# Attention visits merged to one per head pair inside an FFN's matrix products, and the denominators' sums moved to another PSUM bank

## The chip, the cores and the metric

The kernel runs on one core of a Trainium2 chip. Five engines work on it side by side: TensorE (PE in the profile; its weight loads are PEld), VectorE (DVE), ScalarE (ACT), GpSimd (POOL) and SyncE (SP), which issues nearly all the DMA transfers. The metric is the time of one execution on the device in microseconds, the median of several runs.

## The reference

Two stages follow each other. The first is attention with normalized q and k, for 8 batches, 12 heads, 448 rows and 64 columns a head:

```python
def rmsnorm(x, g):
    rms = np.sqrt(np.mean(x * x, axis=-1, keepdims=True) + 1e-06)
    return x / rms * g
q_n, k_n = (rmsnorm(q, g_q), rmsnorm(k, g_k))
scores = scale * np.matmul(q_n, k_n.transpose(0, 1, 3, 2))      # scale = 1 / 8
scores = scores - np.max(scores, axis=-1, keepdims=True)
attn = np.exp(scores)
attn = attn / (np.sum(attn, axis=-1, keepdims=True) + 1e-09)
attn_out = np.matmul(attn, v)
```

Its output is brought to 3584 rows (batch and row) of 768 columns (head and column) and goes through a feed-forward network (FFN) with squared ReLU; `w_in` is 768x2048, `w_out` 2048x768:

```python
h = np.maximum(x @ w_in, 0.0)
out = h * h @ w_out
```

The kernel computes in 32-bit floating point. The FFN's weights come in 64 bits, and the kernel makes 32-bit values of them on the chip.

## The kernel before

**Pairs.** Heads are taken two at a time, which fills 128 partitions with 2 x 64 columns. There are 8 batches of 6 pairs, 48 pairs in all, numbered `i` from 0. A pair's 448 keys are cut into slots `m`: three of 128 keys, and a last half slot of 64, which an even pair shares with the odd pair after it (so an even pair has four slots to score and an odd one three).

**Work of a pair.** Its steps and lines are:

- q and k are squared (`square`, L179 on ScalarE or L181 on GpSimd), added up (`Rows.add`, L192 and L195, VectorE), brought to the power -1/2 (`power`, L202, GpSimd), and q is scaled (`scale`, L217, GpSimd). The factor of k is applied later, as the scale of the exponential.
- q and k are turned, so that the head's columns lie along the partitions. Early pairs do it on TensorE (`turn`, L357 and L360) into a PSUM bank; VectorE takes q out (L365), ScalarE takes k out (L367). Later pairs read 32x32 blocks through DMA, and VectorE turns them in SBUF (`turn_blocks`, L328); ScalarE multiplies q by the gains (L330).
- `weigh`: the scores of a slot for both heads (L387, TensorE, 64 rows by 128 columns of the array for each head; the half slot uses 64 by 64) go to two of the banks 0 to 3, and ScalarE exponentiates them to SBUF (L392). The softmax works without subtracting the maximum when the gains are small enough; that is the branch that runs here (`shift=False`).
- `attend`: weights times v (L458, 128 rows by 64 columns of the array for each head) is summed in the bank of `values_bank`.
- The denominators are sums over keys. In the first phase TensorE forms them (`add_weights`, L471, 128 by 32). Later GpSimd adds the slots up (`add_up`, L411), and TensorE finishes with two products with ones (`denominators`, L488, 128 by 64). They lie in the bank of `sums_bank`.
- VectorE transposes the denominators (`take_sums`, L499), inverts and spreads them (`invert`, L508 to L515) and multiplies the values by them (`finish`, L527), which gives the FFN's input for this pair.

**Stages.** The FFN takes two batches at once in a Strassen scheme of seven products (`first_products` with L646 and L653, `hidden` with L666 to L668, `second_products` with L698, L727 and L768). There are four such FFNs, called units 1 to 4 here; each has four blocks, and a block consists of two times seven products of the first kind (6 matmuls of 448 columns each) and then the second kind (L698 for the rows left over, then 3 times seven products of 4 matmuls of 384 columns each). The FFN uses banks 5, 6 and 7, in turn.

- The *first phase* computes the pairs of batches 0 and 1 without any FFN work, because no input for one is there yet. The weights are converted to 32 bits and to the forms of the Strassen scheme meanwhile (`convert`, L828 to L887, on ScalarE, VectorE and GpSimd).
- *Unit 1* is mixed with the attention of batches 2 and 3, *unit 2* with batches 4 and 5, *unit 3* with 6 and 7. *Unit 4* runs alone.

**What sets the order.** The whole order is written out by hand: the program is emitted with `manual_schedule`, so each engine works in the order of the code. The main loop takes each pair `i` in two *visits* `n` = 0 and 1. In the first phase a visit is `visit_alone`; in the units it is `visit_among`. Between two visits `run` draws steps of the FFN from a generator until a cost is reached (18 for a first product, 10 for a second; a visit comes at every 24th of a unit), and at each step it takes one or two tasks from a queue (`tasks`, `pool_tasks`) of small work of the other engines. What is left of them is emitted at the start of a visit. A visit works on two pairs: it scores slots of pair `i`, and sums values and denominators of pair `i - 1`:

- `visit_alone`, n = 0: scores of slots 0 and 1 of `i`; turn k, then q, of `i + 1` (banks 7 and 6); squares of `i + 2`; three slots of the values of `i - 1`; two slots of its sums (bank 6).
- `visit_alone`, n = 1: the other scores; the last slot of the values; the other two slots of the sums; then `take_sums`, `invert` and `finish`.
- `visit_among`: n = 0 and n = 1 have two slots of values and two slots of scores each, and n = 1 has the denominators (bank 3) ahead of them. From pair 14 on the turn is made by blocks, as two tasks of which one comes ahead of each visit.

A bank with two uses makes a wait: the second writer waits until the first use was read. In the first phase bank 6 serves both the turned q of `i + 1` and the sums of `i - 1`.

Of the kernel before, what the change touches and what calls it, by code (L numbers as in the profile page):

```python
# [21 lines left out]
P = 128  # L22
# [201 lines left out]
def program(ctx, tc, rows, v, g, wide, ones, moe_w_in, moe_w_out, out, shift):  # L224
# [45 lines left out]


    def slots_of(i, n):

        return [m for m in (2 * n, 2 * n + 1) if m < NJ + 1 - i % 2]
# [77 lines left out]
    def turn(i, x):  # L352

        tr = banks[6 + x if i < 2 or alone(i - 2) else 0]
        dst = att.tile([P, S], F32, name="qT" if x == 0 else "kT")
# [22 lines left out]

    def weigh(i, m):

        scs = [banks[m % 2 * 2 + e][:, 0:S] for e in range(2)]
        for p in (i, i + 1) if m == NJ else (i,):
            some = ds(p % 2 * LASTS, LASTS) if m == NJ else ds(0, P)
            keys = ds(m * P, LASTS if m == NJ else P)
            for e, sc in enumerate(scs):
                r = ds(e * D, D)
                nc.tensor.matmul(  # L387
                    sc[some], lhsT=turned[p, 1][r, keys], rhs=turned[p, 0][r, :],
                    start=True, stop=True,
                )  # L390
        for e, sc in enumerate(scs):
            nc.scalar.activation(  # L392
                new_weights((i, m), e), sc, AF.Exp,
                scale=rows.rr[i][:, 1, 2 * m + e : 2 * m + e + 1],
            )
# [46 lines left out]
    def sums_bank(i):  # L442
        return banks[6 if alone(i) else 3][:, 0:S]

# [537 lines left out]
    def weigh_slots(i, n):  # L982
        if not shift:
            for m in slots_of(i, n):
                weigh(i, m)
        elif n:
            weigh_shifted(i)
# [10 lines left out]
    def visit_alone(i, n):  # L998
        step = i * 2 * VISITS + 2 * n
        if n == 0:  # L1000
            load_v(i)
            if i and shift:
                attend_all(i - 1)
            weigh_slots(i, n)
            turn(i + 1, 1)
            turn(i + 1, 0)
            square(i + 2, 0, new_acc())
# [3 lines left out]
            if i and not shift:  # L1011
                attend(i - 1, range(NJ))
                add_weights(i - 1, (0, 1))
                forget(i - 1, (0, 1))
        else:
# [8 lines left out]
            if i and not shift:  # L1024
                attend(i - 1, (NJ,))
                add_weights(i - 1, (2, 3))
                forget(i - 1, (2, 3))
                take_sums(i - 1)
# [14 lines left out]
    def visit_among(i, n):  # L1043
# [15 lines left out]
        if n and i <= last and not shift:  # L1059
            additions(i)  # L1060
        if n == 0 and i + 2 <= last:
            room = io.tile([P, 4 * P], F32, name="squares", tag="squares", bufs=1)
            square(i + 2, 0, room)
            tasks.append(lambda: None)
            tasks.append(lambda: rows.add(i + 2, 0))
            tasks.append(lambda: square(i + 2, 1, room))
            tasks.append(lambda: rows.add(i + 2, 1))
            tasks.append(lambda: pool_tasks.append(lambda: put_in_order(i + 2)))
            if in_blocks(i + 2):
                tasks.append(lambda: load_blocks(i + 2, 1))  # L1070

    with tc.manual_schedule(engines=ENGINES):
# [8 lines left out]
        for i in range(len(pairs) + 1):  # L1081
            for n in range(VISITS):
                at = i * VISITS + n - VISITS - unit
# [4 lines left out]
                if x == 0:  # L1088
                    u, x = u - 1, unit
                run(COST * (2 * x - 1) / (2 * unit))  # L1090
                if i < last:
                    if in_blocks(i + 1):
                        tasks.append(lambda i=i, n=n: turn_blocks(i + 1, 1 - n))
                    else:
                        turn(i + 1, n)
                    if n:
                        tasks.append(lambda i=i: load_qk(i + 4))
# [3 lines left out]
                if x == unit:  # L1101
# [4 lines left out]
                    elif first:  # L1106
                        run(COST_IN + 1)
                visit_among(i, n)
        run(COST)
# [32 lines left out]
```

## Time and profile before

The time before is 1451.85 us, the median of three runs (1451.38 to 1452.49). The profiled execution has a span of 1451.4 us, in which the granted clock of TensorE is 0.999 of full speed.

| stretch, us from the start | what runs | PE busy | DVE busy | ACT busy | POOL busy |
|---|---|---|---|---|---|
| 0 to 140.6 | first phase | 121.7 | 109.4 | 91.3 | 85.2 |
| 140.6 to 503.3 | unit 1, attention of batches 2 and 3 | 359.0 | 245.9 | 194.7 | 217.0 |
| 503.3 to 850.1 | unit 2, attention of batches 4 and 5 | 346.8 | 129.2 | 124.3 | 164.7 |
| 850.1 to 1189.8 | unit 3, attention of batches 6 and 7 | 339.7 | 120.2 | 115.2 | 145.7 |
| 1189.8 to 1446.3 | unit 4 | 255.5 | 69.1 | 59.5 | 31.6 |

A row of a profile's groups has the line of the code, the engine, the operation with what it writes and reads, and how often; in an answer by time the first two numbers are the start and the length in us, and a bracket at the end tells how long the engine had been idle and what released it. Matmuls are pipelined: the recorded length of one contains its run through the array, so a stream of them overlaps, and what one costs is read from the difference between starts. Each matmul instruction of the program stands as two in the trace, so a slot of values for two heads is four rows.

### The profile page before, as it was taken

Reading aid. Unit: us, or ns where it says so; the run is one execution under the profiler, and the core shown is the slowest. Engines: PE = TensorE matmul, PEld = TensorE weight load, DVE = VectorE, ACT = ScalarE, POOL = GpSimd, SP = SyncE. Lnnn points to the kernel's source line nnn. Section 1 sums busy time; section 2 is a strip of 40 time slices with the busy share of each in tenths; the row PEclk is TensorE's granted clock in tenths of the full one; section 3 lists DMA queues with packets and bytes.
Section 4 is the critical chain, followed back from the end, with each engine's and each line's share of the span. In section 5 each row is a group of like instructions: output and inputs, shape, how many; then the busy total and the mean of one; then the engine's idle time right before and its main releaser. Section 6 shows DMA issues by size and latency. Waiting matters only on the chain.

```text
span 1451.4 us, 15319 instructions
## 1 busy us (share of the span) xinstructions
PE 1422.7 (98%) x4932; PEld 680.3 (47%) x4932; DVE 673.8 (46%) x1269; ACT 584.9 (40%) x1102; POOL 644.1 (44%) x568
## 2 busy tenths in 40 slices
PE   7999999999999999999999999999999999999998
PEld 3333444444444445444454444545444455555554
DVE  5898365877768433234352542334234241232313
ACT  5775466647554243432414234352332404222130
POOL 5567654746557545343534645345342422021111
PEclk9999999999999999999999999999999999999999
DMA  5666336665676644525424464343523233223122
GB/s 144 173 190 161 66 96 192 176 193 140 193 202 213 195 127 103 166 74 145 122 64 151 120 189 121 123 100 92 161 66 110 85 120 117 88 76 125 38 87 79
DMA packets 309278, 188.11 MB, mean 130 GB/s; under 512 B 265796, under 2 KB 293316, under 8 KB 300996
## 3 DMA queue, kind: packets, MB, share of 16 engines
q1 hardware_dynamic: 308896, 186.97, 44.2%
q8 instruction: 41, 0.67, 0.2%
q14 instruction: 49, 0.40, 0.1%
q10 hardware_dynamic: 292, 0.07, 0.0%
HBM read 144.57 MB, written 42.40 MB: 129 GB/s over the span
## 4 chain that ended last, share of the span: by engine, by line
PE 93%; DVE 4%; issue 1%; ACT 1%; DMA 1%; POOL 0%; SPq 0%; ACTq 0%; DVEq 0%; POOLq 0%
PE bank L646 35%; PE bank L727 30%; PE bank L387 9%; PE bank L458 9%; PE bank L698 5%; PE bank L488 2%; PE bank L471 1%; DVE few L508 1%; DVE in_sb L865 0%; DVE out_sb L887 0%; DVE inverse L515 0%; DVE in_sb L861 0%; DVE in_sb L841 0%; PE bank L357 0%; DVE qT L365 0%
## 5 line engine op out<-in xcount | busy, mean ns | idle before, releaser
L646 PE MATMUL bank<-xT,in_sb 128*128 128x448 f32 x1344 | 517.5, 542 | 0.0
L646 PEld LDWEIGHTS bank<-xT,in_sb 128*128 128x128 f32 x1344 | 251.7, 190 | 262.4 <-issue 249.4
L768 DVE TENSOR_TENSOR acc<-acc,bank 128x384 f32<-128x384 f32 x324 | 173.7, 549 | 277.0 <-PE bank L727 203.2
L392 ACT ACTIVATE wT<-bank,rr 128x448 f32<-128x448 f32 x288 | 161.5, 633 | 263.9 <-PE bank L387 246.7
L727 PE MATMUL bank<-out_sb,hid 128*128 128x384 f32 x768 | 267.3, 488 | 0.0
L202 POOL TENSOR_TENSOR rr<-ms,minus_half 128x8 f32<-128x8 f32 (+1 forms) x96 | 146.4, 1525 | 249.7 <-DVE ms L195 238.8
L666 DVE TENSOR_TENSOR hid<-bank,part 128x448 f32<-128x448 f32 x128 | 77.0, 622 | 304.1 <-PE bank L646 302.8
L727 PE MATMUL bank<-out_sb,sums 128*128 128x384 f32 x576 | 204.0, 490 | 3.4 <-DVE acc L768 3.3
L727 PEld LDWEIGHTS bank<-out_sb,hid 128*128 128x128 f32 x768 | 144.8, 190 | 106.9 <-issue 6.1
L682 POOL TENSOR_TENSOR sums<-hid 128x384 f32<-128x384 f32 x32 | 32.5, 1016 | 318.2 <-ACT hid L668 318.2
L411 POOL TENSOR_TENSOR sum<-sum,wT 128x448 f32<-128x448 f32 (+1 forms) x144 | 163.6, 1159 | 16.2 <-ACT wT L392 13.8
L387 PE MATMUL bank<-qT,kT 64*128 64x448 f32 (+1 forms) x768 | 163.6, 573 | 1.4 <-DVE qT L365 1.1
L667 ACT ACTIVATE hid<-hid 128x448 f32<-128x448 f32 x128 | 73.4, 574 | 200.4 <-DVE hid L666 200.4
L727 PEld LDWEIGHTS bank<-out_sb,sums 128*128 128x128 f32 x576 | 107.6, 190 | 88.0 <-DVE acc L768 8.4
L653 ACT COPY part<-bank 128x448 f32<-128x448 f32 x128 | 67.9, 530 | 180.0 <-PE bank L646 179.8
L411 POOL TENSOR_TENSOR sum<-wT 128x448 f32<-128x448 f32 x72 | 83.5, 1179 | 71.8 <-PE bank L488 71.8
L458 PE MATMUL bank<-wT,vt 128*64 128x448 f32 x480 | 106.2, 546 | 0.0
L387 PEld LDWEIGHTS bank<-qT,kT 64*128 64x128 f32 (+1 forms) x768 | 55.2, 173 | 106.3 <-issue 86.9
L192 DVE TENSOR_REDUCE ms<-squares 128x8 f32<-128x512 f32 (+1 forms) x68 | 42.0, 617 | 126.3 <-ACT squares L179 126.3
L698 PE MATMUL bank<-out_sb,hid 128*128 128x384 f32 x256 | 86.4, 491 | 0.0
L668 ACT ACTIVATE hid<-hid 128x448 f32<-128x448 f32 x128 | 74.0, 578 | 4.1
L698 PEld LDWEIGHTS bank<-out_sb,hid 128*128 128x128 f32 x256 | 47.6, 190 | 39.3 <-issue 5.7
(83 smaller groups left out, 1135.4 us busy)
## 6 DMA issues: line engine op xcount, KB each, us to landing
out_sb<-out_forms SPq DMA_DIRECT2D x24, 1536.0 KB, 7.6
in_sb<-in_forms SPq DMA_DIRECT2D x24, 1344.0 KB, 5.9
words<-in_moe_w_in_dram SPq DMA_DIRECT2D x32, 384.0 KB, 3.7
words<-in_moe_w_out_dram SPq DMA_DIRECT2D x32, 384.0 KB, 3.6
out_forms<-out_sb SPq DMA_DIRECT2D x8, 1536.0 KB, 6.8
in_forms<-in_sb SPq DMA_DIRECT2D x8, 1344.0 KB, 6.1
qk<-in_q_dram SPq DMA_DIRECT2D x96, 96.0 KB, 3.2
qk<-in_k_dram SPq DMA_DIRECT2D x96, 96.0 KB, 2.7
```

The lines of the kernel that those rows point to most:

```text
L202: self.nc.gpsimd.tensor_tensor(out=self.rr[i][:, x, 0 : self.count(i)], in0=ms, in1=self.minus_half.to_broadcast(list(ms.shape)), op=ALU.pow,)
L387: nc.tensor.matmul(sc[some], lhsT=turned[p, 1][r, keys], rhs=turned[p, 0][r, :], start=True, stop=True,)
L392: nc.scalar.activation(new_weights((i, m), e), sc, AF.Exp, scale=rows.rr[i][:, 1, 2 * m + e : 2 * m + e + 1],)
L411: nc.gpsimd.tensor_tensor(out=sums[i, e][some], in0=left[some], in1=weights[key_of(i, m), e][some], op=ALU.add)
L458: nc.tensor.matmul(values_bank(i)[ds(e * D, D), :], lhsT=lasts[i % 2][mine, e, :] if m == NJ else values[i][:, m, e, :], rhs=weights[key_o ...
L646: nc.tensor.matmul(ps, lhsT=w_sb[:, IN.index(left), c, :], rhs=forms[u, c][right], start=first and c == 0, stop=c == NK - 1, skip_group_ch ...
L666: nc.vector.tensor_tensor(out=dst, in0=left, in1=right, op=op)
L667: nc.scalar.activation(dst, dst, AF.Relu)
L668: nc.scalar.activation(dst, dst, AF.Square)
L698: nc.tensor.matmul(ps, lhsT=flat[a][:, t, ds(NT * P, P)], rhs=w_sb[t][:, 2 * a + half, :], start=(a, t) == parts[0], stop=(a, t) == parts[-1],
L727: nc.tensor.matmul(ps, lhsT=lefts[left][:, t, ts(tt, P)], rhs=w_sb[t][:, OUT.index(right), :], start=first and t == 0, stop=t == 1, skip_g ...
L768: nc.vector.tensor_tensor(out=acc, in0=acc, in1=ps, op=ALU.add)
```

## The change

Four things are changed.

- *From pair 25 on one visit a pair* (`whole`, `visit_whole`), which is from the start of unit 2. The scores of slots 0 and 1 come first, then all values of pair `i - 1`, with the exponentials between them in the order of ScalarE, then the denominators, then the scores of the other slots. The scores lie in banks 0 to 3 in another order (`banks_of`), and the denominators in bank 0. Scoring on TensorE and exponentials are split into `score` and `weigh`. The purpose is that the array's form changes less often.
- *Preparation* (squares, sums of squares, powers, stores of q, loads of blocks) becomes a function, `prepare`, and for the whole visits it is done for pair `i + 3` in place of `i + 2`. The two tasks of the turn come together, half a period ahead of a visit.
- *In the first phase* the sums of a pair lie in the bank of the other parity's values (4 or 5) and no longer in bank 6. TensorE adds them in one group a pair, in the second visit.
- *The order of turning* in the first phase is q and then k, and their banks are 7 and 6.

The diff, cut to its core:

```diff
@@ -269,6 +269,11 @@
+    def whole(i):
+        return i > 2 * 2 * NPAIR
     def slots_of(i, n):
         return [m for m in (2 * n, 2 * n + 1) if m < NJ + 1 - i % 2]
@@ -351,7 +356,7 @@
     def turn(i, x):
-        tr = banks[6 + x if i < 2 or alone(i - 2) else 0]
+        tr = banks[7 - x if i < 2 or alone(i - 2) else 0]
         dst = att.tile([P, S], F32, name="qT" if x == 0 else "kT")
         for j in range(NJ):
             nc.tensor.transpose(
@@ -376,9 +381,14 @@
             weights[n, e] = att.tile([P, S], F32, name="wT", tag="wT", bufs=8)
         return weights[n, e]
-    def weigh(i, m):
-        scs = [banks[m % 2 * 2 + e][:, 0:S] for e in range(2)]
+    def banks_of(i, m):
+        first = 2 * m - 3 if whole(i) and m > 1 else m % 2 * 2
+        return [banks[(first + e) % 4][:, 0:S] for e in range(2)]
+    def score(i, m):
+        scs = banks_of(i, m)
         for p in (i, i + 1) if m == NJ else (i,):
             some = ds(p % 2 * LASTS, LASTS) if m == NJ else ds(0, P)
             keys = ds(m * P, LASTS if m == NJ else P)
@@ -388,7 +398,10 @@
                     sc[some], lhsT=turned[p, 1][r, keys], rhs=turned[p, 0][r, :],
                     start=True, stop=True,
                 )
-        for e, sc in enumerate(scs):
+    def weigh(i, m):
+        for e, sc in enumerate(banks_of(i, m)):
             nc.scalar.activation(
                 new_weights((i, m), e), sc, AF.Exp,
                 scale=rows.rr[i][:, 1, 2 * m + e : 2 * m + e + 1],
@@ -440,7 +453,7 @@
                 nc.vector.tensor_copy(out=tiles[NJ][e][mine, part], in_=tr[mine, NJ, :size])
     def sums_bank(i):
-        return banks[6 if alone(i) else 3][:, 0:S]
+        return banks[4 + (i + 1) % 2 if alone(i) else 0 if whole(i + 1) else 3][:, 0:S]
     def values_bank(i):
         return banks[4 + i % 2 if alone(i) else 4][:, 0:S]
@@ -982,6 +995,7 @@
     def weigh_slots(i, n):
         if not shift:
             for m in slots_of(i, n):
+                score(i, m)
                 weigh(i, m)
         elif n:
             weigh_shifted(i)
@@ -1002,16 +1016,14 @@
             if i and shift:
                 attend_all(i - 1)
             weigh_slots(i, n)
+            turn(i + 1, 0)
             turn(i + 1, 1)
-            turn(i + 1, 0)
             square(i + 2, 0, new_acc())
             square(i + 2, 1, new_acc(), nc.gpsimd)
             begin(step)
             normalize(i + 2, 0)
             if i and not shift:
                 attend(i - 1, range(NJ))
-                add_weights(i - 1, (0, 1))
-                forget(i - 1, (0, 1))
         else:
             weigh_slots(i, n)
             normalize(i + 2, 1)
@@ -1023,8 +1035,8 @@
             load_qk(i + 4)
             if i and not shift:
                 attend(i - 1, (NJ,))
-                add_weights(i - 1, (2, 3))
-                forget(i - 1, (2, 3))
+                add_weights(i - 1, range(NJ + 1))
+                forget(i - 1, range(NJ + 1))
                 take_sums(i - 1)
                 invert(i - 1)
                 finish(i - 1)
@@ -1058,16 +1070,57 @@
             tasks.append(lambda: finish(i - 1))
         if n and i <= last and not shift:
             additions(i)
-        if n == 0 and i + 2 <= last:
-            room = io.tile([P, 4 * P], F32, name="squares", tag="squares", bufs=1)
-            square(i + 2, 0, room)
-            tasks.append(lambda: None)
-            tasks.append(lambda: rows.add(i + 2, 0))
-            tasks.append(lambda: square(i + 2, 1, room))
-            tasks.append(lambda: rows.add(i + 2, 1))
-            tasks.append(lambda: pool_tasks.append(lambda: put_in_order(i + 2)))
-            if in_blocks(i + 2):
-                tasks.append(lambda: load_blocks(i + 2, 1))
+        if n == 0:
+            prepare(i + 2)
+            run_tasks(2)
+            tasks.appendleft(lambda: None)
+        elif whole(i + 1):
+            prepare(i + 3)
+    def prepare(i):
+        if i > last:
+            return
+        room = []
+        tasks.append(
+            lambda: room.append(io.tile([P, 4 * P], F32, name="squares", tag="squares", bufs=1))
+        )
+        for x in range(2):
+            tasks.append(lambda x=x: square(i, x, room[0]))
+            tasks.append(lambda x=x: rows.add(i, x))
+        tasks.append(lambda: pool_tasks.append(lambda: put_in_order(i)))
+        if in_blocks(i):
+            tasks.append(lambda: load_blocks(i, 1))
+    def visit_whole(i):
+        run_tasks(len(tasks) + len(pool_tasks))
+        if i <= last and not shift:
+            for m in slots_of(i, 0):
+                score(i, m)
+        if shift:
+            attend_all(i - 1)
+        else:
+            for n in range(NJ + 1):
+                attend(i - 1, (n,))
+                forget(i - 1, (n,))
+                if i <= last and n < 2:
+                    weigh(i, n)
+            denominators(i - 1)
+        if i <= last:
+            weigh_slots(i, 1)
+            load_v(i)
+        if not shift:
+            tasks.append(lambda: invert(i - 1))
+            tasks.append(lambda: finish(i - 1))
+            if i <= last:
+                additions(i)
+        prepare(i + 3)
+    def turn_among(i, x):
+        if in_blocks(i):
+            tasks.append(lambda: turn_blocks(i, x))
+        else:
+            turn(i, x)
     with tc.manual_schedule(engines=ENGINES):
         if shift:
@@ -1079,7 +1132,7 @@
         if shift:
             rows.scale(1, 1, nc.gpsimd)
         for i in range(len(pairs) + 1):
-            for n in range(VISITS):
+            for n in range(1 if whole(i) else VISITS):
                 at = i * VISITS + n - VISITS - unit
                 if at < 0:
                     visit_alone(i, n)
@@ -1087,13 +1140,11 @@
                 u, x = divmod(at, unit)
                 if x == 0:
                     u, x = u - 1, unit
-                run(COST * (2 * x - 1) / (2 * unit))
+                run(COST * (2 * x - (2 if whole(i - 1) else 1)) / (2 * unit))
                 if i < last:
-                    if in_blocks(i + 1):
-                        tasks.append(lambda i=i, n=n: turn_blocks(i + 1, 1 - n))
-                    else:
-                        turn(i + 1, n)
-                    if n:
+                    for some in (1, 0) if whole(i) else (1 - n,):
+                        turn_among(i + 1, some)
+                    if n or whole(i):
                         tasks.append(lambda i=i: load_qk(i + 4))
                     if n and first and x > 1 and not shift:
                         denominators(i - 1)
@@ -1105,7 +1156,10 @@
                         run(COST)
                     elif first:
                         run(COST_IN + 1)
-                visit_among(i, n)
+                if whole(i):
+                    visit_whole(i)
+                else:
+                    visit_among(i, n)
         run(COST)
         drain()
         for _ in ffn(B // 2 - 1):
```

## Prediction

> **What bounds the kernel now.** I read the busy shares first, then TensorE's waits, then the order of time around the visits that the change touches.
>
> ```profile
> PE 1422.7 (98%) x4932; PEld 680.3 (47%) x4932; DVE 673.8 (46%) x1269; ACT 584.9 (40%) x1102; POOL 644.1 (44%) x568
> ```
>
> TensorE is busy 98% of the span, so only two things can shorten the kernel: the few waits of TensorE, and time that counts as busy but is not needed. TensorE's own list of waits shows the first:
>
> ```profile
> PE bank L471 <- DVE qT L365: 7.5, 5, 1.8
> PE bank L357 <- ACT g L100: 3.5, 1, 3.5
> PE bank L727 <- DVE acc L768: 3.3, 4, 1.3
> ```
>
> The largest item, 7.5 us in 5 waits, is in the first phase (12 pairs, no FFN yet; the first FFN matmul starts at 140.8 us). The sums of a pair (L471) share bank 6 with the turned q of the pair after the next (L357, evacuated by VectorE at L365), and so wait for VectorE. One of the five, and what VectorE does then:
>
> ```profile
> 52.50 0.92 PE L458 MATMUL bank<-acc,vt 128*64 128x448 f32 x4
> 55.17 0.57 PE L471 MATMUL bank<-wT,ones_of 128*32 128x448 f32 x2 [1.75 <-DVE qT L365]
> ```
>
> ```profile
> 54.44 0.67 DVE L365 TENSOR_SCALAR qT<-bank,g 128x448 f32<-128x448 f32 x1
> ...
> 59.88 0.65 DVE L499 STREAM_TRANSPOSE inverse<-bank 128x448 f32<-128x448 f32 x1 [1.06 <-PE bank L471]
> ```
>
> VectorE comes late to q, TensorE idles 1.75 us, and the lost time comes back to VectorE five microseconds later, which idles 1.06 us for the sums (L499). How near VectorE itself is to its limit shows in the windows (columns: length, then busy time of PE, PEld, DVE, ACT, POOL):
>
> ```profile
> 40.00:120.00 80.00, 72.78 (x440) 25.15 (x440) 73.26 (x159) 57.46 (x111) 45.59 (x38) 1.00 0.67 185
> ```
>
> VectorE is as full as TensorE there: 73.3 of 80 us.
>
> The second thing, time that counts as busy, shows in the start times of TensorE's stream within a unit that has FFN work:
>
> ```profile
> 643.27 1.45 PE L727 MATMUL bank<-out_sb,hid 128*128 128x384 f32 x4
> 644.66 0.97 PE L458 MATMUL bank<-wT,lasts 128*64 128x448 f32 x4
> 645.46 0.92 PE L458 MATMUL bank<-wT,vt 128*64 128x448 f32 x4
> 646.31 1.77 PE L387 MATMUL bank<-qT,kT 64*128 64x448 f32 x8
> 648.01 1.56 PE L727 MATMUL bank<-out_sb,sums 128*128 128x384 f32 x4
> 649.41 0.81 PE L727 MATMUL bank<-out_sb,hid 128*128 128x384 f32 x2
> ```
>
> Read differences of starts. Undisturbed, four 128*128 matmuls of 384 columns take 1.29 us, and one step of attention (two 128*64 or two 64*128 matmuls side by side) 0.375 us. Here the four FFN matmuls ahead of the visit take 1.39 (+0.10), the values' four steps 1.65 (+0.15), the scores' four 1.70 (+0.20), the first FFN group after them 1.40 (+0.11). A visit thus loses about 0.55 us at changes of the array's form. A visit with scores for two half slots (64*64) has one change more: its three groups start at 658.53, 659.34 and 660.94, the FFN again at 662.80, and it loses 0.71. There are 48 visits from 499.5 us on, two for each of the pairs from number 25.
>
> **The Trainium skill.** "TensorEngine Tiling (Array Packing)", Key Properties, says that changing the tiling mode, not just the tile, drains TensorE. The trace agrees, at about 0.1 us at each end of a change. "PSUM — Partial Sum Buffer", the section on bank collisions, has PSUM guarded by bank and quadrant, not by address; so a bank with two uses is a wait between them, as bank 6 shows. "SBUF — State Buffer", "SBUF: two separate sides", says that GpSimd and a VectorE operation with two SBUF inputs or in a 2-port mode lock each other out. The trace fits that: one L841 took 1.19 us at 74.89 and another 0.36 at 67.15. So VectorE's 73.3 us is partly waiting inside its instructions, which the change doesn't remove.
>
> **The change, part by part.** The built program has the same 2520 matmuls, and the same number of compute instructions on every engine; only order, banks and waits move.
>
> *One visit a pair (pairs 25 to 48).* Removed: two visits at 0.55 + 0.55 = 1.10 us for an odd pair, 0.55 + 0.71 = 1.26 for an even one. Added: one visit whose order in the program is FFN, scores of two slots, all values and denominators (one form), the other scores, FFN. Its changes: FFN to 64*128 (not in the trace of before; between 0.10, one end, and 0.20, the way back; I take 0.20), 64*128 to 128*64 (likewise, 0.10 to 0.20; I take 0.15, as from FFN), 128*64 to 64*128 (0.20), back to FFN (0.20): 0.75, and 0.16 more for even pairs. Saved: 0.35 a pair, x23 = 8.1 us. The last pair (48) has no scores: two visits at 0.35 (FFN to 128*64 and back) become one, 0.35. Sum 8.4.
>
> *Turning earlier.* In every fourth even pair a visit now falls right behind a product that occupies ScalarE, and the second half slot needs a q that is scaled within the visit:
>
> ```profile
> 544.57 2.28 PE L387 MATMUL bank<-qT,kT 64*128 64x448 f32 x12
> ...
> 545.17 0.66 ACT L330 ACTIVATE qT<-qT,g 128x448 f32<-128x448 f32 x1
> ...
> 545.88 0.20 PEld L387 LDWEIGHTS bank<-qT,kT 64*64 64x64 f32 x4 [0.16 <-ACT qT L330]
> ```
>
> These twelve take 2.21 us to the next start (546.78), against 1.86 at 660.94: 0.35, four times, 1.4 us. With one visit the turn is put down half a period ahead, so I count all of it. Units 2 and 3 together: 9.8 us.
>
> *New waits in the whole visit.* The later scores take banks 1, 2, 3 and 0, which within the same visit held the early scores and, in bank 0, the sums. Queued behind a late one are the scores and then all the FFN. With T the last FFN start, the values start at T+2.2, the first weights can be exponentiated at T+3.1 (their buffers come free with the first values), and four at 0.53 end by T+5.3, or by T+5.7 where four activations of a product (done by T+3.6) come first. The denominators need bank 0 at T+5.2, the later scores need the others at T+6.0 and T+7.0: slack about 0.7 us or more. Bank 0 once more: denominators end, plus 0.07 and 0.65 for the transpose (as at 659.3), plus 0.05 to be seen, 0.77; TensorE wants it after 0.87. That is 0.1 us of slack, 11 times. I take zero, and keep 0.4 us a pair as the other end.
>
> *The FFN between visits.* It loses the visit in the middle of each block, behind which sums on GpSimd and activations had time. Nothing of TensorE's waits in unit 4 (after 1189.6), which has no visits, so I take zero.
>
> *First phase.* One change to the 128*32 form less a pair: 12 x 0.10 = 1.2 us. The wait for bank 6 goes: up to 7.5. But VectorE does the same work. Between 38.9 and 120.7 us (eight pairs, from one L499 to another) it is busy 74.3 of 81.8 us, and its chained small operations leave about 0.56 us a pair between them, 4.5; that leaves 3.0 to be gained while VectorE is the limit. Before that stretch TensorE's wait at 32 us (1.25) counts, after it VectorE is at 15.1 of 20 us and the wait of 1.8 at 125 counts. 3.0 + 1.3 + 1.8, less 0.5 as q is now turned first and must be scaled by GpSimd 0.4 us sooner: 5.6 us. Bounds: 2 (VectorE gives nothing) and 8.7 (all). New: the values of pair i now wait for the transposed sums of i-1 in their bank; between lie four score steps and eight transposes, some 2.9 us, against 0.65 for the transpose. This binds only where VectorE is behind, which the bound by VectorE already holds.
>
> Sum: 9.8 + 5.6 = 15.4; 1451.85 - 15.4 = 1436.5 us.
>
> **The rivals.**
> 1. *TensorE bounds the first phase alone.* For it: five waits name bank 6. Against: the 73.3 us. It gives 9.8 + 8.7 = 18.5: 1433.3.
> 2. *The wait moves.* VectorE remains the limit, and TensorE waits for q at L387 or for the transposed sums at L458 in place of L471. For it: VectorE's share. Against: it idles 6.5 us at L499 in that phase. It gives 9.8 + 2: 1440.
> 3. *Bank 0 or ScalarE costs 0.4 us a whole visit,* 24 x 0.4 = 9.6 of the gain: 1446.
> 4. *Slower.* Each whole visit waits over 1 us for ScalarE or VectorE, or the FFN stalls where it lost its visit: 24 x 1.0 = 24 against 15.4: 1460. For it: exponentials, weights' buffers and banks now form one chain within one visit. Against: the slack above.
>
> **How the numbers follow.** Forecast 0.55, rival 1 0.13, rival 2 0.20, rival 3 0.05, rival 4 0.07. The range takes in rivals 1 and 2 and the bounds of the first phase, and part of what lies between 2 and 3: 1432.5 to 1443. Faster is all but rival 4 and the edge of 3: 0.91; same 0.02, slower 0.07.
>
> **What would show it.** Right: L471 no longer waits for q; 24 visits in units 2 and 3, each with about 0.75 us over its steps; both units together 9 to 10 us shorter, and the first FFN matmul at about 135 us. Wrong: the wait under another name (L458 for L499, L387 for L365) with VectorE over 95% busy; waits of L387 for the transpose of the sums in even pairs; waits of L698 or L727 for ScalarE or GpSimd in the middle of a block.

## The result, and the profile after

The changed kernel takes 1441.41 us (median of four runs, 1440.57 to 1442.67) against 1451.62 for the kernel before in the same comparison: the ratio is 0.9927, interval 0.9911 to 0.9943. That is 10.2 us less; the forecast was 15.4 less. In the changed kernel the lines move down: the turns are L362 and L365, q's evacuation is L370, the scores L397, the exponentials L405, the values L471, the first phase's sums L484, the denominators L501, the FFN's second kind L740.

The busy shares first, then all of TensorE's waits (waited for: us in total, times, longest), of the changed kernel:

```profile
PE 1413.8 (98%) x4932; PEld 685.7 (48%) x4932; DVE 670.8 (47%) x1269; ACT 586.0 (41%) x1102; POOL 644.7 (45%) x568
```

```profile
PE bank L362 <- DVE ms L195: 3.5, 1, 3.5
PE bank L740 <- DVE acc L781: 3.3, 4, 1.3
PE gains L95 <- DVE g_rows L86: 3.2, 1, 3.2
PE bank L471 <- DMA lasts<-in_v_dram: 2.7, 1, 2.7
PE bank L362 <- POOL qk L217: 2.4, 3, 1.3
PE bank L362 <- DVE qk L217: 1.4, 1, 1.4
PE bank L397 <- DVE qT L370: 1.1, 1, 1.1
PE bank L501 <- ACT wT L405: 0.7, 1, 0.7
PE bank L397 <- ACT wT L405: 0.3, 1, 0.3
```

The largest item of before, 7.5 us of the sums for q, is gone. In its place stand 2.7 us of the values for a transfer (1.6 before) and 2.4 us of the turn of q for GpSimd's scaling (0.5 before); in this profile neither is put down to VectorE. The two lines of before:

```profile
PE bank L458 <- DMA lasts<-in_v_dram: 1.6, 1, 1.6
...
PE bank L357 <- POOL qk L217: 0.5, 1, 0.5
```

TensorE's busy time fell by 8.9 us with the same instructions, most of it time that was busy but not needed. Its place is in the order of time (start, length) of a whole visit of an odd pair:

```profile
553.51 1.45 PE L740 MATMUL bank<-out_sb,hid 128*128 128x384 f32 x4
554.90 1.77 PE L397 MATMUL bank<-qT,kT 64*128 64x448 f32 x8
556.60 2.48 PE L471 MATMUL bank<-wT,vt 128*64 128x448 f32 x12
558.91 0.92 PE L471 MATMUL bank<-wT,lasts 128*64 128x448 f32 x4
559.66 0.92 PE L501 MATMUL bank<-sum,ones 128*64 128x448 f32 x4
560.51 1.02 PE L397 MATMUL bank<-qT,kT 64*128 64x448 f32 x4
561.46 1.56 PE L740 MATMUL bank<-out_sb,sums 128*128 128x384 f32 x4
562.86 3.39 PE L740 MATMUL bank<-out_sb,hid 128*128 128x384 f32 x10
```

By differences of starts: the FFN's four matmuls 1.39 (0.10 over 1.29), the scores' four steps 1.70 (+0.20), the ten steps of values and denominators 3.91 (+0.16), the two late score steps 0.95 (+0.20), the FFN again 1.40 (+0.11). Over all visits the loss is about 0.75 us for an odd pair, 0.91 for an even one and 0.35 for the last, with no wait in any. It goes with the form and not with the operands: from the values of `lasts` to the denominators operands and bank change but the form doesn't, and the two steps ahead of that border take 0.75 us (558.91 to 559.66), no more than undisturbed ones.

The windows over 40 to 120 us, where the forecast had VectorE as the limit (length, then busy time of PE, PEld, DVE, ACT, POOL, then the granted clock):

```profile
40.00:120.00 80.00, 75.21 (x446) 27.33 (x446) 71.96 (x157) 57.73 (x110) 48.23 (x39) 0.98 0.72 195
```

VectorE is less full than before (72.0 against 73.3 of 80 us), not fuller.

Where the time went, from the starts of the units' first FFN matmuls in the two traces (the changed kernel's profiled execution was the slowest of its four):

| stretch | before, us | after, us | difference |
|---|---|---|---|
| first phase | 140.75 | 137.38 | -3.4 |
| unit 1 | 362.54 | 366.47 | +3.9 |
| units 2 and 3 | 686.54 | 673.60 | -12.9 |
| unit 4, to VectorE's last operation | 256.50 | 256.51 | 0 |
| from there to the end | 5.12 | 6.83 | +1.7 |

One correction belongs to this table. The visit of pair 25 stands ahead of unit 2's first matmul. As a whole visit it has 16 steps and takes 3.2 us longer than the half visit that stood there. So 3.2 us of the 12.9 are only work moved over the border: units 2 and 3 gain 9.7, and unit 1 loses 0.7, the new wait at L501. That wait comes with the first phase's part of the change: it is 0.7 us in the run with the first phase alone and 0.2 in the one with the whole visits alone.

### The profile page after: what moved, and what is told of

It reads as the page before. It is cut to its first block, busy times and chain, and to the rows that moved or that the text cites. A ratio compares the mean times of both kernels' runs of the same rounds, so it can differ in the third digit from the quotient of the medians.

```text
span 1440.8 us, 15368 instructions
## 1 busy us (share of the span) xinstructions
PE 1413.8 (98%) x4932; PEld 685.7 (48%) x4932; DVE 670.8 (47%) x1269; ACT 586.0 (41%) x1102; POOL 644.7 (45%) x568
## 4 chain that ended last, share of the span: by engine, by line
PE 93%; DVE 2%; DMA 1%; ACT 1%; POOL 1%; issue 1%; SPq 0%; ACTq 0%; POOLq 0%; DVEq 0%
PE bank L659 34%; PE bank L740 30%; PE bank L471 10%; PE bank L397 9%; PE bank L711 5%; PE bank L501 2%; PE bank L484 1%; PE bank L362 1%; POOL rr L202 0%; ACT wT L405 0%; DMA q_rows<-qk 0%; DVE out_sb L900 0%; DVE acc L781 0%; DVE in_sb L878 0%; DMA words<-in_moe_w_out_dram 0%
## 5 line engine op out<-in xcount | busy, mean ns | idle before, releaser
L740 PE MATMUL bank<-out_sb,hid 128*128 128x384 f32 x768 | 266.5, 487 | 0.0
L405 ACT ACTIVATE wT<-bank,rr 128x448 f32<-128x448 f32 x288 | 160.8, 631 | 124.3 <-PE bank L397 78.2
L740 PE MATMUL bank<-out_sb,sums 128*128 128x384 f32 x576 | 204.0, 490 | 3.4 <-DVE acc L781 3.3
L740 PEld LDWEIGHTS bank<-out_sb,hid 128*128 128x128 f32 x768 | 145.5, 190 | 103.6 <-issue 1.4
L397 PE MATMUL bank<-qT,kT 64*128 64x448 f32 (+1 forms) x768 | 164.3, 574 | 1.7 <-DVE qT L370 1.1
L680 ACT ACTIVATE hid<-hid 128x448 f32<-128x448 f32 x128 | 73.3, 572 | 191.7 <-DVE hid L679 191.7
L740 PEld LDWEIGHTS bank<-out_sb,sums 128*128 128x128 f32 x576 | 107.7, 190 | 88.1 <-DVE acc L781 8.4
L397 PEld LDWEIGHTS bank<-qT,kT 64*128 64x128 f32 (+1 forms) x768 | 55.1, 174 | 104.8 <-issue 67.6
L471 PE MATMUL bank<-wT,vt 128*64 128x448 f32 x480 | 102.2, 546 | 0.0
L512 DVE STREAM_TRANSPOSE inverse<-bank 128x448 f32<-128x448 f32 x48 | 31.0, 646 | 118.8 <-PE bank L501 111.8
L335 ACT ACTIVATE qT<-qT,g 128x448 f32<-128x448 f32 x34 | 22.6, 666 | 141.4 <-DVE qT L333 141.4
```

Of the source, the lines that this page charges most:

```text
L397: nc.tensor.matmul(sc[some], lhsT=turned[p, 1][r, keys], rhs=turned[p, 0][r, :], start=True, stop=True,)
L405: nc.scalar.activation(new_weights((i, m), e), sc, AF.Exp, scale=rows.rr[i][:, 1, 2 * m + e : 2 * m + e + 1],)
L471: nc.tensor.matmul(values_bank(i)[ds(e * D, D), :], lhsT=lasts[i % 2][mine, e, :] if m == NJ else values[i][:, m, e, :], rhs=weights[key_o ...
L680: nc.scalar.activation(dst, dst, AF.Relu)
L740: nc.tensor.matmul(ps, lhsT=lefts[left][:, t, ts(tt, P)], rhs=w_sb[t][:, OUT.index(right), :], start=first and t == 0, stop=t == 1, skip_g ...
```

## The experiments

Times are medians; each ratio is against the kernel before, run on the same chip. "The changed kernel" is the base unless the text says before.

**The whole visits alone.** The changed kernel with the first phase of before.

```diff
-        tr = banks[7 - x if i < 2 or alone(i - 2) else 0]
+        tr = banks[6 + x if i < 2 or alone(i - 2) else 0]
-        return banks[4 + (i + 1) % 2 if alone(i) else 0 if whole(i + 1) else 3][:, 0:S]
+        return banks[6 if alone(i) else 0 if whole(i + 1) else 3][:, 0:S]
...
```

> Only the one visit a pair from pair 25 on; the first phase as before. Theory (the array's changes of form are what units 2 and 3 gave): units 2 and 3 become 9.7 us shorter as in the changed kernel, the first phase stays at 140.8 us, so about 1442 us, or 1443.5 if the wait for instructions at the end is there too. Rival (units 2 and 3 gained because the first phase changed how VectorE and GpSimd enter them): under 7 us from these units.

Measured: 1443.68 us, ratio 0.9937 (0.9924 to 0.9951). Units 2 and 3 take 673.60 us, to the hundredth what they take in the changed kernel; the first phase ends at 140.65. The old wait is back, under its old cause:

```profile
PE bank L484 <- DVE qT L370: 7.2, 5, 1.8
```

The two halves of the change hardly act on each other: this one gains 9.2 us and the next one 4.2, and the changed kernel without its late end (the padded kernel below, same chip) gains 14.3.

**The first phase alone.** The same from the other side: no pair is whole.

```diff
-        return i > 2 * 2 * NPAIR
+        return i > len(pairs)
```

> Only the first phase's part: sums in the bank of the other parity's values, in one group, q turned first; two visits a pair everywhere. Theory (the parts are independent): first FFN matmul at 137.4 us in place of 140.8, units 2 and 3 as before, 1448 us, give or take the wait at the end. Rival: the first phase gains nothing by itself, 1451.5.

Measured: 1448.67 us, ratio 0.9970 (0.9961 to 0.9980). Units 2 and 3 are as before (686.51). The first FFN matmul starts at 135.95, 4.8 us earlier than before, where the changed kernel's profile had 3.4 earlier.

**More changes of form.** In a whole visit the scores of slot 1 come after the second slot of values, which adds two changes of form and no work.

```diff
-            for m in slots_of(i, 0):
-                score(i, m)
+            score(i, 0)
...
+                if i <= last and n == 1:
+                    score(i, 1)
                 if i <= last and n < 2:
                     weigh(i, n)
```

> The changed kernel with the scores of slot 1 put between the second and third slot of the values in each whole visit: the same matmuls, two changes of the array's form more (to 64*128 and back). Theory (a change costs what the starts show): 0.35 us for each of 23 pairs, 8.1 us more than the changed kernel, about 1449.5. Rival (the gain of a whole visit comes from fewer interruptions of the FFN, or from waits, and not from the changes): within 1.5 us of the changed kernel.

Measured: 1449.09 us, ratio 0.9974 (0.9965 to 0.9984). Units 2 and 3 take 681.34 us, 7.74 more. They hold 22 of the changed visits (that of pair 25 stands ahead of unit 2, that of pair 48 has no scores), so each costs 0.352 us more. In the same visit of its trace, the inserted scores:

```profile
555.56 1.30 PE L471 MATMUL bank<-wT,vt 128*64 128x448 f32 x6
556.79 1.02 PE L397 MATMUL bank<-qT,kT 64*128 64x448 f32 x4
557.74 0.97 PE L471 MATMUL bank<-wT,vt 128*64 128x448 f32 x4
558.55 0.92 PE L471 MATMUL bank<-wT,lasts 128*64 128x448 f32 x4
```

Two score steps (0.75 us) take 0.95. So the gain of the whole visits goes with the count of changes of form, and the price is 0.35 us for two.

**Turning earlier, alone.** The kernel before, with both tasks of a turn ahead of its first visit.

```diff
-                        tasks.append(lambda i=i, n=n: turn_blocks(i + 1, 1 - n))
+                        for x_ in (1, 0) if n == 0 else ():
+                            tasks.append(lambda i=i, x_=x_: turn_blocks(i + 1, x_))
```

> The kernel before, with both tasks of a pair's turn put down ahead of the first visit in place of one ahead of each. Theory (a part of what the whole visits gave, 1.4 us, was the late q of every fourth even pair): units 2 and 3 become 1.4 us shorter, and unit 1 by up to 4 us, since five of its six even pairs lose 0.5 to 1.1 us more than 0.71 in their second visit. Rival (those second visits wait for something else): no gain in either, 1451.9.

Measured: 1451.75 us against 1453.34, ratio 0.9990 (0.9982 to 0.9999). Units 2 and 3 are 1.37 us shorter, which is the forecast term of 1.4. Unit 1 gains only 0.67 of the up to 4 that were expected: by the starts, the second visits of its even pairs lose 4.2 us less, but other visits and the FFN behind them lose most of it again, with new waits:

```profile
PE bank L646 <- DVE acc L768: 2.0, 2, 1.5
...
PE bank L488 <- ACT wT L392: 1.1, 1, 1.1
```

Unit 1 seems to have little room for work that moves earlier; two runs below return to this.

**The bank alone.** The kernel before, in which the sums of the first phase lie in the bank of the other parity's values, still in two groups and with the old order of turning.

```diff
-        return banks[6 if alone(i) else 3][:, 0:S]
+        return banks[4 + (i + 1) % 2 if alone(i) else 3][:, 0:S]
```

> The kernel before with the first phase's sums in the bank of the other parity's values, and nothing else: still two groups, k turned first. Theory (the group in the first visit would come while that bank's values are still being read at L527, behind VectorE's inversion, so the change of bank needs the one group): the wait of L471 for q at L365 becomes one for L527, first FFN matmul at 139 us or later. Rival (the bank alone is what helps): first FFN matmul at 136.0.

Measured: 1449.15 us, ratio 0.9978 (0.9971 to 0.9984); first FFN matmul at 137.62. TensorE's waits for the values and the sums in it:

```profile
PE bank L458 <- DMA lasts<-in_v_dram: 2.9, 1, 2.9
...
PE bank L471 <- DVE xT L527: 1.6, 2, 1.3
```

The wait did move to the multiplication of the values (L527), whose bank the sums now take, but shrank from 7.5 to 1.6 us. The expectation that most of it would come back was wrong: the bank alone brings the first FFN matmul 3.1 us forward. The run with k turned first below has the single group too and otherwise the same first phase; it starts the FFN at 135.97, so the single group is worth 1.7 us more. (In both the granted clock was halved for 3.41 us at about 111 us, as told at the end.)

**The transfer of v.** What bounds the first phase now? The wait of 2.7 us in the changed kernel, TensorE (start, length, and in brackets the idle time and its releaser):

```profile
107.60 0.27 PE L365 MATMUL bank<-wide,qk 128*128 128x128 f32 x1
110.61 0.97 PE L471 MATMUL bank<-wT,lasts 128*64 128x448 f32 x4 [2.74 <-DMA lasts<-in_v_dram]
111.38 1.54 PE L471 MATMUL bank<-part,vt 128*64 128x448 f32 x4
112.64 1.77 PE L471 MATMUL bank<-acc,vt 128*64 128x448 f32 x4
```

SyncE's queue in the same kernel:

```profile
98.55 0.34 SPq L902 DMA_DIRECT2D out_forms<-out_sb  x1
...
106.66 1.23 SPq L342 DMA_DIRECT2D vt<-in_v_dram  x2
107.93 0.62 SPq L347 DMA_DIRECT2D lasts<-in_v_dram  x1
```

The store of a converted weight (L902) had waited 4.3 us for GpSimd (L900); behind it stand eight loads of q and k, and only then the loads of v, which the values need at 107.9. The two steps from 111.38 on cost 1.26 us in place of 0.75: the half clock described at the end. In some other profiles (the repetition, the padded kernel, more changes of form) the same wait is put down to VectorE's L528, which ends just ahead of the values' start, so a run has to decide. The experiment puts the loads of v ahead of those of q and k, in the visit before.

```diff
         if n == 0:
-            load_v(i)
+            if i == 0:
+                load_v(i)
...
+            if (i + 1) * VISITS - VISITS - unit < 0:
+                load_v(i + 1)
             load_qk(i + 4)
```

> The changed kernel with the loads of v for the next pair issued in the first phase's second visit, ahead of the loads of q and k, in place of at the start of the next visit. Theory (the wait for the last rows of v at 107 us, 2.5 us, comes of SyncE's order of issue, and is what keeps the first phase behind the forecast): that wait goes, first FFN matmul at 134 us or a little after. Rival (VectorE is the limit in that stretch and takes the time back): the wait goes, first FFN matmul still within 0.7 us of 136.0.

Measured: 1436.38 us, ratio 0.9884 (0.9869 to 0.9900); first FFN matmul at 133.43. The load is now issued six microseconds earlier, and the values follow the turn without a wait:

```profile
101.54 1.33 SPq L347 DMA_DIRECT2D lasts<-in_v_dram  x1
```

```profile
107.31 0.27 PE L365 MATMUL bank<-wide,qk 128*128 128x128 f32 x1
107.51 0.97 PE L471 MATMUL bank<-wT,lasts 128*64 128x448 f32 x4
```

The values start at 107.51, and VectorE's L528 for this pair ends only at 109.33, so they never needed it. At this place it was SyncE's order, not VectorE, that held TensorE back. The store itself was not the cause: it still stands ahead of v and waits even longer (5.8 us). What moved are the eight loads between.

**k turned first.** The changed kernel with the old order of turning.

```diff
-            turn(i + 1, 0)
             turn(i + 1, 1)
+            turn(i + 1, 0)
```

> The changed kernel with the old order of turning in the first phase (k, then q). Theory (turning q first makes TensorE wait for GpSimd's scaling of q, 2.4 to 3.0 us in all, but VectorE and the transfers bound that phase anyway): the waits for L217 fall by 1 to 2 us, the first FFN matmul comes within 0.7 us of 136.0. Rival (TensorE's waits add up): the first FFN matmul 1.5 us or more earlier, 134.5.

Measured: 1438.52 us, ratio 0.9900 (0.9885 to 0.9915). The first FFN matmul starts at 135.97. TensorE's waits for GpSimd's scaling fall to 0.7 us, from 2.4 in the changed kernel and 3.0 in the padded one below; yet the padded one is as early (136.00). The wait ahead of the values grew, from 2.5 us there to 3.1, but the values after it still start 0.8 us earlier (109.34 against 110.18). Then the clock was halved for 3.41 us, which the padded kernel was spared, and that took the rest. Where v comes early, neither happens: the best kernel below, which has k first and the padding besides, starts the FFN at 131.58 against 133.43, so there the old order gives 1.9 us. This run also ended without the late fetch told of next, so its better time is no proof for the order.

**The end.** The last stretch is 1.7 us longer after, though nothing was changed there. In it one of SyncE's last instructions comes 1.73 us after the one before it, where those ahead followed within 0.1, and an instruction fetch of 8192 bytes falls into that gap. The page's line of the instruction queue (packets, MB, share) counts two more than before, where it was 49:

```profile
q14 instruction: 51, 0.42, 0.1%
```

The experiment adds transfers to a branch that isn't run, so that only the place of SyncE's code in memory moves (a tensor in DRAM that nothing uses comes with them).

```diff
         if shift:
+            for _ in range(12):
+                nc.sync.dma_start(unused, ones)
             rows.scale(0, 1, nc.gpsimd)
```

> The changed kernel with 12 more transfers in the branch that is not run, so that SyncE's instructions at the end stand where they stood in the kernel before. Theory (the 1.7 us between two of SyncE's last waits are a fetch of instructions that falls there by the program's layout): 1.7 us less than the changed kernel, the stretch from the last VectorE operation to the end 5.1 us in place of 6.8. Rival (those 1.7 us wait for the output's transfer or differ from run to run): 6.8 us as before.

Measured: 1438.57 us, ratio 0.9902 (0.9887 to 0.9917). The last stretch is 5.08 us again, and the count is one lower:

```profile
q14 instruction: 50, 0.41, 0.1%
```

Three profiles show 51 packets, and these alone have a last stretch of 6.8 to 7.1 us: the changed kernel, its repetition and the kernel with more changes of form. All others show 49 or 50 and 5.1 us.

**The changed kernel again.** Unedited.

> The changed kernel once more, beside the next ones. Theory (in its first profile 1.4 us of the first phase were a fall of the granted clock after a wait of 2.7 us, which need not come each time; the 1.7 us at the end come each time, by the layout): about 1440 us; the stretch after the last VectorE operation 6.8 us again; first FFN matmul at 136.0 or 137.4 us. Rival (the stretch at the end varies from run to run): 5.1 us at the end.

Measured: 1441.06 us, ratio 0.9920 (0.9907 to 0.9934), last stretch 7.09. The late end repeats. The first FFN matmul starts at 136.03, although the clock was halved for 3.41 us here too (from 109.6 us on), so the halved clock alone, which the expectation names, doesn't explain 137.38. TensorE was also 1.2 us later in the first profile, from about 17 us on. The padded kernel started about as late but kept its clock, and has 136.00. So either of the two gives 136.0, and only both together 137.4: 4.7 us earlier than before is the more typical gain of the first phase.

**Whole visits in unit 1 too.** From pair 14, where the turn by blocks begins; padded against the late end.

```diff
-        return i > 2 * 2 * NPAIR
+        return i > 2 * NPAIR + 1
```

> The changed kernel with whole visits from pair 14 on, so in unit 1 too, and SyncE's instructions at the end where they stood in the kernel before. Theory (the same changes of form are saved, two for each denominators' visit more, and the late q's wait): about 22.9 us of losses in unit 1 become 11, so 10 us or more less than the changed kernel without its late fetch, 1428. Rival (VectorE, ScalarE and GpSimd, which carry the weights' conversion in unit 1, can't follow within one visit): new waits of L501, L397 or L471, and a gain under 4 us.

Measured: 1448.68 us, ratio 0.9968 (0.9956 to 0.9981): 7 us slower than the changed kernel and about 10 slower than the padded one, which is its fair base, where the theory had it faster. The visits did cost what they should, 0.75 and 0.91 us, all but one of them. Yet unit 1 takes 375.88 us against 366.47. Of its TensorE waits:

```profile
PE bank L741 <- DVE acc L782: 10.3, 7, 3.2
PE bank L741 <- POOL out_sb L901: 4.3, 1, 4.3
...
PE bank L741 <- ACT acc L756: 2.0, 1, 2.0
```

They stand in the FFN, not in the visits: 16.6 us in unit 1, against 4.0 in the changed kernel. That is 12.6 more, and TensorE's busy time is 3.0 less; the difference, 9.6, is the loss but for 0.2. The busy time hides a second loss: at three of these waits the granted clock fell to a half, for 6.83, 3.41 and 6.83 us, of which TensorE worked 14.9. By estimate half of that, about 7 us, was lost, so the visits did save the 11 us or so that the theory counted, and waits and clock took almost twice as much.

**The best of it.** The changed kernel with v loaded early, k turned first and the padding.

> The changed kernel with v loaded early, k turned first and SyncE's instructions at the end in the old place. Theory (with the wait for v gone VectorE bounds the first phase, and the waits for L217, 2.3 us, are partly hidden by it): first FFN matmul at 132.5 to 133.4 us, about 1434.5 us. Rival (TensorE bounds it): 131.5 or earlier.

Measured: 1434.45 us, ratio 0.9876 (0.9861 to 0.9891), which beats both kernels; first FFN matmul at 131.58, 9.2 us earlier than before. Its windows over 40 to 120 us and TensorE's waits for the first phase's scores, turns and values:

```profile
40.00:120.00 80.00, 78.11 (x466) 28.46 (x462) 74.98 (x167) 59.48 (x114) 50.96 (x41) 1.00 0.69 192
```

```profile
PE bank L398 <- DVE qT L371: 1.7, 2, 1.1
PE bank L363 <- DVE qk L217: 0.9, 1, 0.9
PE bank L363 <- POOL qk L217: 0.7, 1, 0.7
PE bank L472 <- DVE inverse L513: 0.6, 2, 0.3
```

TensorE is at 78.1 of 80 us and VectorE at 75.0, more than in either kernel, and still VectorE costs TensorE only these few waits. So 131.58 lies at the rival's 131.5 (TensorE bounds the phase) and outside the theory's 132.5 to 133.4, although the time came out as the theory had it.

**The last five pairs of unit 1 as whole visits.** The combined kernel, with whole visits from pair 20.

```diff
-        return i > 2 * 2 * NPAIR
+        return i > 2 * NPAIR + 7
```

> The combined kernel with whole visits from pair 20 on, so in the last five pairs of unit 1 too. Theory (what whole visits lost in unit 1 were the FFN's waits for VectorE and GpSimd while these convert weights; near the end of the unit too much of that is still going on): visits save 4 to 5 us in unit 1, new waits of L741 take more than half of it back, within 2.5 us of the combined kernel. Rival (the conversions are over by then): 4 to 5 us less than it.

Measured: 1444.26 us, ratio 0.9944 (0.9930 to 0.9957), 9.8 us slower than the combined kernel, far more than the 2.5 that the theory allowed. Unit 1 takes 375.57 us against 366.18. TensorE's waits in unit 1:

```profile
PE bank L741 <- DVE acc L782: 6.4, 6, 3.2
PE bank L741 <- POOL out_sb L901: 4.3, 1, 4.3
...
PE bank L502 <- ACT wT L406: 2.6, 2, 2.0
```

13.3 us, against 3.7 in the combined kernel: the difference, 9.6, is the loss of 9.4. Here too two of the waits were followed by the half clock (3.41 and 6.83 us, of which TensorE worked 8.2: about 4 us lost, by estimate), which took what the visits saved. GpSimd during the longest of them, which TensorE leaves at 469.94:

```profile
457.83 1.87 POOL L202 TENSOR_TENSOR rr<-ms,minus_half 128x8 f32<-128x8 f32 x1 [1.89 <-DVE ms L195]
459.67 1.40 POOL L696 TENSOR_TENSOR sums<-hid 128x384 f32<-128x384 f32 x1
...
464.67 1.14 POOL L565 TENSOR_TENSOR xT<-xT 128x448 f32<-128x448 f32 x1
465.75 1.00 POOL L901 TENSOR_TENSOR out_sb<-out_sb 128x384 f32<-128x384 f32 x1
466.70 2.23 POOL L565 TENSOR_TENSOR xT<-xT 128x448 f32<-128x448 f32 x2
468.88 1.01 POOL L901 TENSOR_TENSOR out_sb<-out_sb 128x384 f32<-128x384 f32 x1
```

GpSimd waited for VectorE, then had the FFN's sums, the inputs of the next FFN and the converted weights in one row, and TensorE needed the last of them. That whole visits make the FFN wait in unit 1 is shown, twice. That it is because the small work there has no slack fits the order above, but was not tested by itself, and which rule of the emission puts it late (the preparation for `i + 3`, or the missing draw of tasks at the second visit) was not told apart.

## Why the prediction was right, and where it missed

- *One visit a pair, 8.4, and turning earlier, 1.4: right.* The visits cost 0.75, 0.91 and 0.35 us as forecast, turning earlier gave 1.37 by itself, and units 2 and 3 gained 9.7 for 9.8. The two estimates that the trace of before didn't show (FFN to 64*128 and 64*128 to 128*64) held in their sum. The Trainium skill's statement in "TensorEngine Tiling (Array Packing)", Key Properties, that a change of tiling mode, not just of the tile, drains TensorE, agrees with the run with more changes (0.352 us for two) and with the border without a change of form (nothing).
- *New waits in the whole visit, zero: right.* In units 2 and 3 TensorE's busy time equals their length (341.91 and 331.68 us); rivals 3 and 4 fall.
- *The FFN between visits, zero: right where the change was made,* but the reason given was too general. In unit 1 the same visits made the unit 9.4 us longer, twice, by waits in the FFN and the half clock behind them. The sum also left out the 0.7 us that unit 1 pays at L501, which come with the first phase's part. That units 2 and 3 are spared fits the load of the helpers (VectorE works 128 and 117 us there, GpSimd 165 and 142, against 249 and 222 in unit 1); it was not tested.
- *The first phase, 5.6: this step failed.* It said that 3.0 us are to be gained "while VectorE is the limit". VectorE wasn't: it fell to 72.0 of 80 us in the changed kernel, and went up to 75.0 in the combined one. The phase gained 3.4 us in the profile, 4.7 to 4.8 in most runs; the rest was held by the transfer of v behind the loads of q and k in SyncE's queue (2.6 us, shown by moving the load) and by the scaling of q on GpSimd (waits of 2.4 us, 1.9 more than before, where the sum took off 0.5; with v early the old order gave 1.9). With both out of the way it gained 9.2, a little more than rival 1's bound of 8.7, which had no term for the transfer. So rival 1 named the right limit, TensorE, and the changed kernel ended near rival 2's number (1440) for a reason that rival 2 didn't have. The clue stood in the profile of before: a wait of 1.6 us of L458 for `lasts`, which the prediction didn't read.
- *The end, not in the sum:* 1.7 us for a late fetch of SyncE's instructions, shown by moving its code.

The sum, forecast and by the trace: 9.8 to 9.7, 5.6 to 3.4, and nothing to -0.7 and -1.7: 15.4 to 10.7. That 1441.41 us still lies in the range, 1.6 us from its end at 1443, is partly luck. The range was wide for the sake of VectorE in the first phase and of part of rival 3; what did come, the order of the loads, the scaling of q and the late fetch, was not in it, and one more loss of the fetch's size would have gone beyond it.

## What to carry to other kernels

Count TensorE's changes of array form in an interleaved stream and price them by differences of starts: that forecast was right to a tenth of a microsecond. When a large wait goes, look for the next one in the list of waits, and read the queue of the engine that issues the transfers before you call the engine with the most busy time the limit. A reordering that cost nothing in two stages cost two to three times its gain in a third, where the helpers were busier, so test each stage by itself.

## What the runs showed of the hardware

- *Half clock after a short idle time.* The idle time of TensorE ahead of the values at about 109 us was followed by a granted clock of 0.5 for 3.41 us in four profiles (2.58 us of idle time in the repetition, 2.74 in the changed kernel, 2.89 with the bank alone, 3.06 with k first). In the changed kernel the fall began at 111.6 us, a microsecond after TensorE had restarted. After 2.48, 2.49 and 2.68 us (padded kernel, first phase alone, more changes of form) there was none, yet with whole visits in unit 1 the clock was halved for 6.83 us around an idle time of only 2.43. So length alone doesn't decide: some 3.5 us of idle time at 4 us of the kernel before left its clock at 1.00 as well. The Trainium skill, "TensorE: Matmul & The Clock Gate", Part 1, gives half rate after an idle window of about 3.4 us; the length of the falls (3.41 us or twice that) agrees, but here less recorded idle time was enough. In unit 1 waits of 3.1 to 4.3 us brought falls of 3.41 and 6.83 us (whole visits in unit 1 and from pair 20).
- *A late instruction fetch at the end of a program* cost 1.7 to 2.0 us in three profiles, and went away with more code in a branch that isn't run.
- *Order in SyncE's queue:* eight loads of q and k, issued from 99.4 to 106.6 us, made TensorE wait 2.7 us for a load of v that stood behind them and had nothing to do with them. With v ahead of them the wait was gone, though the store ahead of all of them still waited 5.8 us for GpSimd.
